# From batch 3 on, queries and keys of a batch's first two pairs are asked for behind the second value part of a pair under way

## The chip, the core and the metric

The kernel runs on one core of one Trainium2 chip. The metric is device microseconds from start to end of one launch; the time of a version is the median of several runs. The core has five engines with their own instruction queues: TensorE (PE, with its weight loads listed as PEld), VectorE (DVE), ScalarE (ACT), GpSimd (POOL) and SyncE (SP). In this kernel every DMA is issued by SP, in the order of SP's program, so a DMA that must wait holds all DMAs behind it.

## The reference

Windowed attention over 8 batches, 8 heads, 576 positions and 64 channels; half of the heads look at the last 32 positions, half at every fourth of the last 128. Its output, 8 x 576 x 512, goes through a mixing layer with cosines and sines.

```python
scores = scale * np.matmul(q, k.transpose(0, 1, 3, 2))
scores = np.where(masks[None, :, :, :], scores, -1000000000.0)
attn = softmax(scores); x = np.matmul(attn, v)      # then heads side by side: (B, S, 512)
theta = x @ w_theta
zr, zi = x * np.cos(theta), x * np.sin(theta)
y = einsum('ts,bsd->btd', w_tok_r, zr) + einsum('ts,bsd->btd', w_tok_i, zi)
u = x + y
out = u + np.maximum(u @ w_ch, 0.0)
```

## The kernel before

**Pairs.** Two heads make a pair; a batch has four pairs, 0 to 3 (`NP` = 4). For a pair the kernel loads queries `q` (576 KB), keys `k` (304 KB) and the values of nine windows in two parts: `va`, the first five windows (320 KB), and `vb`, the last four (256 KB). In the names of tiles the batch comes first: `q4_0` is the queries of batch 4, pair 0. There are two buffers for `q`, `k` and `va`, and **one** for `vb`.

**Steps on TensorE.** `scores(b, pr)` (tile `s`, L547) multiplies queries by keys, and `pv(b, pr)` (tile `o`, L704) multiplies the turned probabilities `pt` by the values: 20 matmul records on `va`, then 16 on `vb`. `theta` (tile `th`) is the product with `w_theta`. The token products of a batch are 14 steps (tiles `A`, `B`, `C`, `D`, L1169) on weights that are held in scratch DRAM as `tw_...` and brought into `wt_g`, `late_wt_a` and `late_wt_b` when their turn comes (576 KB a half). `chan` (tile `c`, L1406) is the product with `w_ch`.

**Phases.** From batch 1 on the work runs in phases. Phase b does the 14 steps of batch b, and between them the attention of batch b+1; then `theta` of batch b+1 and `chan` of batch b. From phase 2 on the order on TensorE is: scores(b+1, 2), step 0 (A), pv(b+1, 0), scores(b+1, 3), steps 1 to 3 (B, A, B), pv(b+1, 1), steps 4 and 5 (A), pv(b+1, 2), scores(b+2, 0), steps 6 to 9 (C, D), pv(b+1, 3), scores(b+2, 1), steps 10 to 13 (C, D), and then `theta` and `chan`. So pv(b+1, 1) and pv(b+1, 2) have two steps between them. Phase 1 has the older, slower token product (tile `y`, L1373) in place of the 14 steps, and beside it POOL and ACT build the weight sums `tw_t1` to `tw_t4` (L1071 to L1094), which SP stores (L1100).

**What sets the order.** The steps are Python generators. Each yields an engine and an estimated cost, or an event that it waits for, and `Order.run` works out from that in which order the instructions are written into the engines' programs. A load is such a generator (`load_qk`, `load_va`, `load_vb`): it becomes due when its buffer is freed in that plan, and takes its place in SP's program by its due time. On the chip the engines keep the program order and wait on semaphores. `load_qk` of the pair two further on is started after `scores` of a pair, `load_vb` of the next pair after `pv`. `od.steady` is true once the phases are planned; `FIRST` is 2.

**Names in the prediction.** `x_store` (L842, L849) writes the attention output transposed to DRAM (`xd`) and reads it back as `xn`, in five parts; the part of 64 rows is used first, by the products at L856. `keep` (L1057) stores two weight sets as `tw_b11` and `tw_b22` in phase 1.

Of the kernel before, what the change touches and what calls it, by code (L numbers as in the profile page):

```python
# [58 lines left out]
FIRST = 2  # L59
# [21 lines left out]
class Order:  # L81
# [14 lines left out]
    def pin(self, ins):  # L96
        if self.live:
            self.tc.keep_in_program_order(ins)

    def signal(self, event):  # L100
        self.events[event] = self.now
# [96 lines left out]
def dma(n):  # L198
    return 128 * 4 * n / 360.0
# [3 lines left out]
def build(ctx, tc, qT, kT, vw, wth, wtk, wch, maskb, ident, identb, outT):  # L203
# [14 lines left out]
    od = Order(tc)  # L218
    pin, go, signal = od.pin, od.go, od.signal
# [16 lines left out]
    def reserve(tag):  # L236
        taken[tag] = taken.get(tag, -1) + 1
        return taken[tag]

    def take(tag, bufs, n=None):  # L240
        n = reserve(tag) if n is None else n
        if od.live:
            if n >= bufs:
                yield None, ("free", tag, n - bufs)
            if n:
                yield None, ("got", tag, n - 1)
            signal(("got", tag, n))
        return n
# [15 lines left out]
    def load_qk(n):  # L264
        if n >= B * NP:
            return
        b, pr = divmod(n, NP)
        yield "rank", due.get(("scores", b, pr), od.rank)
        r = yield from take("qk", 2)
        q = ap.tile([128, 2 * NJ, 2 * QB], F32, tag="q", name=f"q{b}_{pr}")  # L270
        k = ap.tile([128, S + 32], F32, tag="k", name=f"k{b}_{pr}")
        yield "DMA", dma(2 * S)
        pin(nc.sync.dma_start(q, qT[b, pr]))
        yield "DMA", dma(S + 32)
        pin(nc.sync.dma_start(k, kT[b, pr]))
        qks[b, pr] = (q, k, r)
        signal(("qk", b, pr))
# [13 lines left out]
    def load_vb(n):  # L291
        if n >= B * NP:
            return
        b, pr = divmod(n, NP)
        yield "rank", due.get(("pv", b, pr), od.rank)
        if n == NP - 1:
            r = None
            vb = hp.tile([128, DM], F32R, tag="zl8", name="first_vb").bitcast(F32)
            vb = vb.rearrange("p (a b) -> p a b", b=128)
        else:  # L300
            r = yield from take("vb", 1)
            vb = ap.tile([128, NJ - VA, 128], F32, tag="vb", name=f"vb{b}_{pr}", bufs=1)
        yield "DMA", dma((NJ - VA) * 128)
        pin(nc.sync.dma_start(vb, vw[b, pr, :, VA:]))
        vs["b", b, pr] = (vb, r)
        signal(("vb", b, pr))
# [38 lines left out]
    def first_loads():  # L345
        yield "DMA", dma(3 * BW + 64)
        pin(nc.sync.dma_start(mskb, maskb.bitcast(BF16)))
        pin(nc.sync.dma_start(idb, identb.bitcast(BF16)))
        for pr in range(NP):
            yield from take(f"xh{pr}", 1, 0)  # L350
            yield from take(f"u{pr}", 1, 0)
            pqs.append(hp.tile([128, 2, S], F32R, tag=f"xh{pr}", name=f"P0_{pr}").bitcast(F32)[:, 0])
            q = hp.tile([128, 2, S], F32R, tag=f"u{pr}", name=f"q0_{pr}").bitcast(F32)
            q = q.rearrange("p a b -> p (a b)").rearrange("p (a b) -> p a b", b=2 * QB)
            k = first_k[:, KE * pr:KE * pr + KE]
            yield "DMA", dma(2 * S)
            pin(nc.sync.dma_start(q, qT[0, pr]))
            yield "DMA", dma(KE)
            pin(nc.sync.dma_start(k, kT[0, pr]))
            qks[0, pr] = (q, k, None)  # L360
            if pr == 0:
                yield "DMA", dma(128)
                pin(nc.sync.dma_start(idt, ident))
            signal(("qk", 0, pr))
        for pr in range(NP // 2):
            v = first_v[:, NJ * 128 * pr:NJ * 128 * pr + NJ * 128].rearrange("p (a b) -> p a b", b=128)
            yield "DMA", dma(NJ * 128)
            pin(nc.sync.dma_start(v, vw[0, pr]))
            for h, t in (("a", v[:, :VA]), ("b", v[:, VA:])):
                vs[h, 0, pr] = (t, None)  # L370
                signal(("v" + h, 0, pr))
        for pr in range(NP // 2, NP):
            yield from load_va(pr)
            yield from load_vb(pr)
# [143 lines left out]
    def scores(b, pr):  # L518
# [36 lines left out]
        if b == 0:  # L555
            give(f"u{pr}", 0)
        else:
            give("qk", rqk)
            go(load_qk(b * NP + pr + 2), RANK["load"])
# [128 lines left out]
    def pv(b, pr):  # L688
        yield None, ("va", b, pr)
        yield None, ("vb", b, pr)  # L690
        yield None, ("pt", b, pr)
        if pr >= 1:
            yield None, ("pv", b, pr - 1)
        if b > 2:
            yield None, ("stored", b - 2, pr)
        (va, ra), (vb, rb) = vs["a", b, pr], vs["b", b, pr]
        xf[b, pr] = xp.tile([128, S], F32, tag=f"x{pr}", name=f"x{b}_{pr}")
        n = yield from take("v", 1)
        ps = ps_v.tile([128, 2 * DM], F32, tag="v", name=f"o{b}_{pr}")[:, :S]
        yield "PE", 1060 if od.steady else 1300  # L700
        for j in range(NJ):
            v = va[:, j] if j < VA else vb[:, j - VA]
            for hh in range(2):
                pe(nc.tensor.matmul(ps[64 * hh:64 * hh + 64, BW * j:BW * j + BW], v[:, 64 * hh:64 * hh + 64],  # L704
                                    pmats[b, pr][:, j, hh], start=True, stop=True))
        go(x_evac(b, pr, ps, ("v", n), ("xe", b, pr)))
        signal(("pv", b, pr))
        n = b * NP + pr
        if ra is not None:
            give("va", ra)  # L710
            go(load_va(n + 2), RANK["load"])
        if rb is not None:
            give("vb", rb)
            go(load_vb(NP if n == NP - 2 else n + 1), RANK["load"])
        if b:
            go(x_split(b, pr))
# [828 lines left out]
    def second_loads():  # L1545
        for n in (NP, NP + 1):
            yield from load_qk(n)
# [113 lines left out]
```

## Time and profile before

| | |
|---|---|
| median of 3 runs | 564.9 us (564.89 to 566.3) |
| the profiled execution's own time | 562.37 us |
| its span | 560.6 us |
| granted TensorE clock, mean | 0.991 |
| busy share: PE, PEld, DVE, ACT, POOL | 95%, 86%, 78%, 66%, 59% |
| DMA queue of SP, share of 16 engines | 64.8%, 123.49 MB |
| phases 2 to 6, first scores to first scores | 61.74, 62.38, 62.11, 62.04, 59.43 us |

The profiled execution is 2.5 us below the median of the runs, and its span is 1.8 us below its own time; differences are worked out on the span and carried over to the median. Phase 6 is shorter since no batch 8 follows, so it has two score steps fewer and loads no queries and keys. A "busy" share counts instructions in flight, so 95% on PE hides short waits; the chain that ended last and the gaps between PE's rows show them.

### The profile page before, as it was taken

How to read it: one execution, taken by the hardware profiler on the slowest of the kernel's cores; microseconds unless marked ns; L12 is line 12 of the kernel's file. 1: busy time of each engine (PE TensorE's matmuls, PEld its weight loads, DVE VectorE, ACT ScalarE, POOL GpSimd, SP SyncE). 2: the span in 40 equal slices, each digit the busy share in tenths (PEclk: the TensorE clock that was granted, in tenths of full speed). 3: DMA queues.
4: the chain of work that ended last, by engine and by line, in shares of the span. 5: the costliest groups of instructions: out<-in, count | busy, mean ns of one | idle time of the engine just before them, and what ended most of it. 6: DMA issues, size and time to landing. Idle time of an engine off the chain costs nothing.

```text
span 560.6 us, 14386 instructions
## 1 busy us (share of the span) xinstructions
PE 530.9 (95%) x5320; PEld 481.5 (86%) x5320; DVE 434.9 (78%) x1315; ACT 372.4 (66%) x1033; POOL 332.5 (59%) x351
## 2 busy tenths in 40 slices
PE   4897799889998999999999999999999999999997
PEld 3744689778997899998999899998999899989997
DVE  3889799994687787979897997979797997748322
ACT  1598966868748578487776778487767767567220
POOL 2228858788994274763567374655476375727660
PEclk9999799899999999999999999999999999999999
DMA  8991535832659948995499918993599817690622
GB/s 303 400 390 29 177 108 185 256 118 96 201 200 309 317 162 324 322 263 189 141 363 292 307 44 314 324 279 149 199 341 290 276 63 227 213 279 37 211 92 85
DMA packets 59126, 124.41 MB, mean 222 GB/s; under 512 B 5424, under 2 KB 24624, under 8 KB 58800
## 3 DMA queue, kind: packets, MB, share of 16 engines
q1 hardware_dynamic: 59056, 123.49, 64.8%
q8 instruction: 42, 0.69, 0.5%
q14 instruction: 28, 0.23, 0.1%
HBM read 99.88 MB, written 23.59 MB: 220 GB/s over the span
## 4 chain that ended last, share of the span: by engine, by line
PE 70%; DVE 9%; DMA 9%; POOL 5%; ACT 4%; issue 2%; SPq 1%; DVEq 0%; POOLq 0%
PE c L1406 16%; PE th L776 12%; PE C L1169 9%; PE D L1169 7%; PE A L1169 5%; PE B L1169 4%; PE s L547 4%; PE o L704 4%; PE y L1373 4%; DMA vb<-in_vw_dram 4%; DMA st_wtk<-in_wtk_dram 3%; DVE pt L608 3%; POOL z L737 1%; DMA first_k<-in_kT_dram 1%; PE th L781 1%
## 5 line engine op out<-in xcount | busy, mean ns | idle before, releaser
L608 DVE STREAM_TRANSPOSE pt<-P 32x288 f32<-32x288 f32 x224 | 105.2, 470 | 11.8 <-POOL P L590 7.3
L1406 PE MATMUL c<-u,late_wc 128*128 128x288 f32 x768 | 108.3, 295 | 0.0
L1406 PEld LDWEIGHTS c<-u,late_wc 128*128 128x128 f32 x768 | 105.6, 188 | 2.6
L584 ACT ACTIVATE P<-P,mx 128x64 f32<-128x64 f32 x216 | 72.3, 336 | 12.7 <-DVE mx L578 12.5
L776 PE MATMUL th<-wthh,xh 128*128 128x512 f32 x224 | 74.9, 395 | 0.0
L590 POOL TENSOR_TENSOR P<-P,sm 128x576 f32<-128x576 f32 x32 | 39.5, 1235 | 59.0 <-DVE mx L578 29.4
L1187 POOL TENSOR_TENSOR u<-x,u 128x288 fp32r<-128x288 f32 x48 | 40.1, 838 | 20.8 <-ACT u L1185 20.6
L1185 ACT CAST u<-x 128x288 fp32r<-128x288 f32 x48 | 20.5, 427 | 45.0 <-DVE x L1195 45.0
L776 PEld LDWEIGHTS th<-wthh,xh 128*128 128x128 f32 x224 | 42.1, 188 | 9.2
L776 PE MATMUL th<-wthl,xh 128*128 128x512 f32 x112 | 44.3, 396 | 0.0
L486 DVE CUSTOM_DVE_ANT_0 P<-s,mskb 128x64 f32<-128x64 f32 x216 | 33.2, 217 | 14.3 <-PE s L547 14.3
L584 ACT ACTIVATION_READ_ACCUMULATOR P<-P,mx 128x1 f32 x216 | 40.4, 187 | 0.0
L664 ACT COPY x<-o 128x576 f32<-128x576 f32 x32 | 29.5, 921 | 15.0 <-PE o L704 14.9
L737 POOL TENSOR_TENSOR zl<-g,zh 128x512 fp32r<-128x512 f32 x7 | 9.1, 1297 | 48.9 <-ACT zh L735 48.9
L1382 DVE SCALAR_TENSOR_TENSOR x<-c,x 128x288 f32<-128x288 f32 x64 | 28.3, 449 | 12.3 <-PE c L1406 12.2
L547 PE MATMUL s<-k,q 128*64 128x64 f32 x1008 | 36.6, 226 | 0.0
L547 PEld LDWEIGHTS s<-k,q 128*64 128x64 f32 x1008 | 32.8, 140 | 3.7 <-issue 2.7
L704 PEld LDWEIGHTS o<-pt,va 128*64 128x64 f32 x600 | 21.4, 140 | 7.2 <-issue 4.9
L949 POOL TENSOR_TENSOR s<-f,x 128x256 f32<-128x256 f32 x24 | 17.8, 740 | 16.1 <-DVE f L937 13.7
L704 PE MATMUL o<-pt,va 128*64 128x64 f32 x600 | 25.6, 230 | 1.7 <-ACT pt L622 1.2
L1373 PE MATMUL y<-wt_g,z 128*128 128x288 f32 x96 | 20.7, 320 | 6.7 <-POOL z L737 4.1
L776 PEld LDWEIGHTS th<-wthl,xh 128*128 128x128 f32 x112 | 21.0, 188 | 4.0
(245 smaller groups left out, 1609.4 us busy)
## 6 DMA issues: line engine op xcount, KB each, us to landing
q<-in_qT_dram SPq DMA_DIRECT2D x32, 576.0 KB, 5.8
late_wt_a<-tw_t SPq DMA_DIRECT2D x24, 576.0 KB, 6.2
wt_g<-tw_b SPq DMA_DIRECT2D x22, 576.0 KB, 6.1
va<-in_vw_dram SPq DMA_DIRECT2D x30, 320.0 KB, 5.6
k<-in_kT_dram SPq DMA_DIRECT2D x28, 304.0 KB, 6.0
out_dram<-x SPq DMA_DIRECT2D x28, 288.0 KB, 2.1
vb<-in_vw_dram SPq DMA_DIRECT2D x29, 256.0 KB, 4.5
xd<-xq SPq DMA_DIRECT2D x24, 288.0 KB, 5.3
```

The costliest lines, as they stand in the source:

```text
L486: pin(nc.vector.tensor_tensor_reduce(out=P[:, n], in0=ps[:, n - g0], in1=mskb[:, mask_of(pr, n)], op0=ALU.add, op1=ALU.max, scale=1.0, sca ...
L547: pe(nc.tensor.matmul(ps[64 * e:64 * e + 64, n - g0], q[:, qb], k[:, QB * qb:QB * qb + BW], start=not masked, stop=not masked or n == g1 - 1))
L584: table(nc.scalar.activation(P[:, n], P[:, n], AF.Exp, bias=mx[:, n:n + 1], scale=SCALE, accum_out=sm[:, n:n + 1]))
L590: pin(nc.gpsimd.tensor_tensor(P, P, sm.unsqueeze(2).to_broadcast([128, NJ, BW]), op=ALU.mult))
L608: pin(nc.vector.transpose(pmats[b, pr][k0:k0 + QB, :, hh, QB * e:QB * e + QB], P[p0:p0 + QB, :, QB * o:QB * o + QB]))
L664: pin(nc.scalar.copy(dst, src))
L704: pe(nc.tensor.matmul(ps[64 * hh:64 * hh + 64, BW * j:BW * j + BW], v[:, 64 * hh:64 * hh + 64], pmats[b, pr][:, j, hh], start=True, stop=T ...
L776: pe(nc.tensor.matmul(pt, l, r, start=(n == 0), stop=(n == 3 * NC - 1)))
L1169: pe(nc.tensor.matmul(ps, l, r, start=first and n == 1, stop=last and n == 3 * len(ks), skip_group_check=more))
L1187: pin(nc.gpsimd.tensor_tensor(ul[b, d][:, ts], x[:, ts], uh[b, d][:, ts].bitcast(F32), op=ALU.subtract))
L1373: pe(nc.tensor.matmul(ps, l[:, cs], r, start=(n == 0), stop=(n == 3 * NK - 1)))
L1406: pe(nc.tensor.matmul(ps, l[:, cs], r[:, ts], start=(n == 0), stop=(n == 3 * NC - 1)))
```

## The change

A load of queries and keys for pair 0 or 1 of batch 3 or later, after its buffer number is given out, now also waits in the plan until `load_vb` of (batch before, pair + 1) has taken the `vb` buffer. So `q4_0` and `k4_0` are planned behind `vb3_1`, and `q4_1` and `k4_1` behind `vb3_2`. No instruction is added or taken away, and no buffer changes; the change acts only through the order in which `Order.run` writes the programs.

```diff
         r = yield from take("qk", 2)
+        if od.steady and b > FIRST and pr < 2:
+            yield None, ("vbi", b - 1, pr + 1)
         q = ap.tile([128, 2 * NJ, 2 * QB], F32, tag="q", name=f"q{b}_{pr}")
...
             r = yield from take("vb", 1)
+            signal(("vbi", b, pr))
             vb = ap.tile([128, NJ - VA, 128], F32, tag="vb", name=f"vb{b}_{pr}", bufs=1)
```

The order on PE stays as it was. SP's order changes in phases 1 to 5, and DVE, ACT and POOL change theirs at the end of phase 1 alone. The added lines move later line numbers by 2 or 3.

**SP, first part of phase 2** (phases 3, 4 and 5 move alike). Before:

```order
L273 DMA q4_0_2779<-in_qT_dram 128x1152
L275 DMA k4_0_2780<-in_kT_dram 128x608
L1051 DMA wt_g_90<-tw_t3_1491 128x1152
L304 DMA vb3_1_2840<-in_vw_dram 128x512
L287 DMA va3_2_2839<-in_vw_dram 128x640
L273 DMA q4_1_2865<-in_qT_dram 128x1152
L275 DMA k4_1_2866<-in_kT_dram 128x608
L1051 DMA wt_g_90<-tw_t3_1491 128x1152
L304 DMA vb3_2_2972<-in_vw_dram 128x512
L287 DMA va3_3_2971<-in_vw_dram 128x640
L1051 DMA late_wt_a_788<-tw_t4_1529 128x1152 x2
```

And now:

```order
L1054 DMA wt_g_90<-tw_t3_1491 128x1152
L307 DMA vb3_1_2836<-in_vw_dram 128x512
L289 DMA va3_2_2835<-in_vw_dram 128x640
L275 DMA q4_0_2837<-in_qT_dram 128x1152
L277 DMA k4_0_2838<-in_kT_dram 128x608
L1054 DMA wt_g_90<-tw_t3_1491 128x1152
L307 DMA vb3_2_2968<-in_vw_dram 128x512
L289 DMA va3_3_2967<-in_vw_dram 128x640
L275 DMA q4_1_2969<-in_qT_dram 128x1152
L277 DMA k4_1_2970<-in_kT_dram 128x608
L1054 DMA late_wt_a_788<-tw_t4_1529 128x1152
L307 DMA vb3_3_3046<-in_vw_dram 128x512
```

`q4_0` and `k4_0` moved from ahead of `vb3_1` to behind `va3_2`, `q4_1` and `k4_1` from ahead of `vb3_2` to behind `va3_3`; further on `q4_2` and `k4_2` went behind the two halves of `tw_b22`, and `va4_1` behind `k4_3`.

**SP in phase 1, around the last value part of batch 2** (`tx`, `ta`, `tb`, `tc`, `td` are the tiles in which POOL and ACT leave the weight sums). Before:

```order
L1100 DMA tw_t3_1491<-tb_1803 128x288
L1100 DMA tw_t3_1491<-ta_1802 128x288
L1100 DMA tw_t2_1511<-tx_102 128x288 x2
L1100 DMA tw_t2_1511<-tc_1804 128x288
L1100 DMA tw_t2_1511<-tb_1803 128x288
L1100 DMA tw_t4_1529<-tx_102 128x288
L1100 DMA tw_t4_1529<-td_1805 128x288
L1100 DMA tw_t4_1529<-ta_1802 128x288
L304 DMA vb2_3_2163<-in_vw_dram 128x512
L1100 DMA tw_t4_1529<-tx_102 128x288
L273 DMA q3_2_2194<-in_qT_dram 128x1152
```

And now:

```order
L277 DMA k3_1_2022<-in_kT_dram 128x608
L1103 DMA tw_t3_1491<-tb_1803 128x288
L1103 DMA tw_t3_1491<-ta_1802 128x288
L1103 DMA tw_t3_1491<-tx_102 128x288
L1103 DMA tw_t2_1511<-tc_1804 128x288
L1103 DMA tw_t2_1511<-tb_1803 128x288
L1103 DMA tw_t3_1491<-tx_102 128x288
L1103 DMA tw_t4_1529<-td_1805 128x288
L1103 DMA tw_t4_1529<-ta_1802 128x288
L307 DMA vb2_3_2161<-in_vw_dram 128x512
L1103 DMA tw_t2_1511<-tx_102 128x288 x2
L1103 DMA tw_t4_1529<-tx_102 128x288 x2
```

`k3_1` now stands among the stores (`q3_1` three rows above it), and of the stores from `tx` three more stand behind `vb2_3` than before.

**SP at the end of phase 1, the return of the attention output of batch 2.** Before:

```order
L273 DMA q3_3_2312<-in_qT_dram 128x1152
L842 DMA xd2_2321<-xq2_2220 32x18x128 x4
L275 DMA k3_3_2313<-in_kT_dram 128x608
L849 DMA xn2_2421<-xd2_2321 64x512
L1057 DMA tw_b11_2484<-wt_g_90 128x2304
L1057 DMA tw_b22_2505<-late_wt_b_994 128x2304
L849 DMA xn2_2421<-xd2_2321 128x512 x4
```

And now:

```order
L275 DMA q3_3_2310<-in_qT_dram 128x1152
L845 DMA xd2_2324<-xq2_2235 32x18x128 x4
L277 DMA k3_3_2311<-in_kT_dram 128x608
L289 DMA va3_1_2278<-in_vw_dram 128x640
L1060 DMA tw_b11_2480<-wt_g_90 128x2304
L1060 DMA tw_b22_2503<-late_wt_b_994 128x2304
L852 DMA xn2_2423<-xd2_2324 64x512
L852 DMA xn2_2423<-xd2_2324 128x512 x4
```

The read of the 64-row part of `xn2` moved behind the two stores of 1152 KB each, `tw_b11` and `tw_b22`.

## The prediction

> **What bounds the kernel now.** I read the page first, then who waits for whom on PE, then the chain that ended last phase by phase, and last SP's rows with the time from issue to landing of single DMAs.
>
> ```profile
> span 560.6 us, 14386 instructions
> PE 530.9 (95%) x5320; PEld 481.5 (86%) x5320; DVE 434.9 (78%) x1315; ACT 372.4 (66%) x1033; POOL 332.5 (59%) x351
> PE 70%; DVE 9%; DMA 9%; POOL 5%; ACT 4%; issue 2%; SPq 1%; DVEq 0%; POOLq 0%
> PE o L704 <- DMA vb<-in_vw_dram: 3.7, 5, 2.2
> ```
>
> PE bounds the kernel, and its own work stays as it is. What the change can touch is the last row: `pv` waits five times for `vb`, 3.7 us in all, the longest 2.2 us. A gap between PE's rows understates a stall, since matmuls overlap, so I measure it on the chain. There each phase from 2 to 6 has the same piece: step 4 and 5 (A, 24 records), then pv(b+1, 2), then what follows.
>
> ```profile
> 223.26 3.38 PE A L1169 x24
> 226.65 1.56 PE o L704 x36
> ...
> 285.04 4.82 DMA vb<-in_vw_dram
> 290.58 1.05 PE s L547 x36
> ...
> 300.20 1.05 PE s L547 x36
> ...
> 347.44 4.54 DMA vb<-in_vw_dram
> 352.71 1.05 PE s L547 x36
> ...
> 409.53 4.49 DMA vb<-in_vw_dram
> 414.75 1.05 PE s L547 x36
> ...
> 471.53 3.38 PE A L1169 x24
> 474.92 1.35 PE o L704 x36
> ```
>
> In phases 3, 4 and 5 the chain leaves PE and runs over the DMA of `vb`, issued the moment pv(b+1, 1) frees the only buffer. From that moment to the end of pv(b+1, 2) it is 4.95 us in phase 2 (226.65 + 1.56 - 223.26), 5.54 in phase 3 (290.58 - 285.04), 5.27 in phase 4, 5.22 in phase 5, and 4.74 in phase 6 (474.92 + 1.35 - 471.53). Phase 6 loads no queries and keys, so it is the price without them. Above it stand 0.21, 0.80, 0.53 and 0.48 us: 2.02 us in four phases.
>
> The latest time at which `vb` costs nothing is read from PE's own rows:
>
> ```profile
> 289.89 0.69 PE L704 MATMUL o<-pt,vb 128*64 128x64 f32 x16 [0.62 <-DMA vb<-in_vw_dram]
> ...
> 475.53 0.22 PE L704 MATMUL o<-pt,vb 128*64 128x64 f32 x1
> ```
>
> In phase 6 the first matmul on `vb` starts 4.0 us after the issue (475.53 - 471.57, row below). In phase 3 it starts 0.04 us after the landing (285.04 + 4.82 = 289.86).
>
> **Why `vb` lands late.** SP's rows of phase 3, and of phase 6 last:
>
> ```profile
> 276.39 0.53 SPq L273 DMA_DIRECT2D q<-in_qT_dram  x1
> 276.98 0.46 SPq L275 DMA_DIRECT2D k<-in_kT_dram  x1
> 277.53 0.38 SPq L1051 DMA_DIRECT2D wt_g<-tw_t  x1
> 278.00 0.38 SPq L304 DMA_DIRECT2D vb<-in_vw_dram  x1
> 278.44 0.80 SPq L287 DMA_DIRECT2D va<-in_vw_dram  x1
> 279.32 0.43 SPq L273 DMA_DIRECT2D q<-in_qT_dram  x1
> 279.80 0.46 SPq L275 DMA_DIRECT2D k<-in_kT_dram  x1
> 282.24 0.33 SPq L1051 DMA_DIRECT2D wt_g<-tw_t  x1
> 285.04 0.33 SPq L304 DMA_DIRECT2D vb<-in_vw_dram  x1
> ...
> 471.57 0.33 SPq L304 DMA_DIRECT2D vb<-in_vw_dram  x1
> ```
>
> And the time to landing (last number, us) of single issues: the `q` of 276.39, the `k` of 279.80, the `wt_g` of 282.24, and the `vb` of 471.57 in phase 6.
>
> ```profile
> q<-in_qT_dram SPq DMA_DIRECT2D x1, 576.0 KB, 4.3
> k<-in_kT_dram SPq DMA_DIRECT2D x1, 304.0 KB, 8.0
> wt_g<-tw_t SPq DMA_DIRECT2D x1, 576.0 KB, 7.0
> vb<-in_vw_dram SPq DMA_DIRECT2D x1, 256.0 KB, 2.6
> ```
>
> So they land at 280.7, 287.8, 289.2, and the `vb` of 285.04 at 289.86: in the order of issue, a queue. From 280.7 to 289.86 seven DMAs behind the first `q` and the last `vb` itself land: 304 + 576 + 256 + 320 + 576 + 304 + 576 + 256 = 3168 KB in 9.2 us, 345 KB a microsecond. With nothing queued `vb` takes 2.6 us.
>
> **The change, part by part.**
>
> *Phases 2 to 5, `q` and `k` of the first pair behind `vb` and `va`, those of the second behind the next `vb`.* The same transfers run, but ahead of the `vb` of 285.04 there is now one `q` and `k` instead of two, 880 KB less: 880 / 345 = 2.55 us. Worked out forward: `wt_g` goes first and lands where the first `q` did, 280.7; `vb`, `va`, `q`, `k` (1456 KB, 4.2 us) by 284.9; the second `wt_g` (1.7 us) by 286.6; `vb` by 287.3, and not before 285.04 + 2.6 = 287.6. The deadline is 285.04 + 4.0 = 289.0, so 1.4 us are to spare and the stall goes. Phases 2, 4 and 5 were less late and have the same queue. Term: -2.02 us. If pv(b+1, 2) came down to the 1.20 us that the chain gives every other `pv` of a phase, it would be 0.15 more in each of four phases, -2.6 in all; I don't take that, since phase 6 keeps its 1.35 though its `vb` landed at 474.2, before it was needed. The other end is 0 (rival 1).
>
> *What is late next there.* `q` and `k` of the first pair are issued at about 279 to 280, as the second pair's were, and their slowest landing before was 8.0 us: 287.8, with scores at 290.58 now and about 289.8 then. Cover of 2 us at the old backlog, 4.5 at the new one (284.9): cost 0. Those of the second pair are issued behind `va` at about 286, land by 294 at the slowest, and their scores start at 300.20 in phase 3. Cost 0. `late_wt_a`, 880 KB further back, is read at step 10 still later, and its second half now also stands behind the wait of `vb3_3` on pv(b+1, 2); both are past by 291. `q` and `k` of the third pair now wait behind both halves of `tw_b22` (the end of step 7), some 4 us later for work of the next phase, which is 40 us off. `va` of the second pair moves behind `xn`, again for a use some 30 us off.
>
> *Phase 1, `vb2_3` among the stores.* pv(2, 3) has the longest stall of all:
>
> ```profile
> 165.72 1.74 SPq L1100 DMA_DIRECT2D tw_t<-tc  x1
> ...
> 169.51 0.40 SPq L304 DMA_DIRECT2D vb<-in_vw_dram  x1
> ...
> 167.07 1.26 POOL L1094 TENSOR_TENSOR ta<-ta,td 128x288 fp32r<-128x288 f32 x1
> ...
> 169.63 0.80 PE L704 MATMUL o<-pt,va 128*64 128x64 f32 x20 [0.51 <-ACT x L664]
> 172.63 0.69 PE L704 MATMUL o<-pt,vb 128*64 128x64 f32 x16 [2.19 <-DMA vb<-in_vw_dram]
> ```
>
> `vb2_3` was issued at 169.51 and landed 3.1 us later. It stays behind the store of `ta`, which waits for POOL until 167.07 + 1.26 = 168.33. Then follow `ta` and `vb`, at half a microsecond an issue: 168.9 at best, if SP isn't behind. It may be: the 1.74 us of the `tc` issue can come again (its cause isn't in the trace), and then `vb` goes out at about 169.6. Three stores fewer stand ahead, but 880 KB of `q3_1`, `k3_1` now run in this stretch. Landing 2.6 to 3.1 us after the issue: 171.5 to 172.7, against 172.6. The term lies between -1.1 and +0.1; I take -0.5, the middle.
>
> *End of phase 1, the 64-row part of `xn2` behind 2304 KB of stores.* This is the part that can cost:
>
> ```profile
> tw_b<-late_wt_b SPq DMA_DIRECT2D x1, 1152.0 KB, 7.8
> ...
> 193.94 0.68 DVE L856 TENSOR_TENSOR g<-xn,th 64x512 f32<-64x512 f32 x1
> 204.37 0.69 DVE L856 TENSOR_TENSOR x<-xn,th 128x512 f32<-128x512 f32 x1 [0.29 <-ACT f L911]
> ...
> 203.07 7.99 PE c L1406 x60
> ```
>
> The second store was issued at 185.95, so it landed at 193.8; the part of `xn2` now lands right behind it, 194.2 to 194.9, where DVE read it at 193.94 before. DVE may stand still up to 1.0 us. Behind it on DVE are the sums on `c` and the products that free PSUM banks; the nearest need is the bank that the third `chan` unit of the last run takes: it starts two units behind 203.07, 7.99 / 5 = 1.6 us each, at 206.3, and the product that frees its bank ended at 204.37 + 0.69 = 205.1. Cover 1.2 us, so cost 0; at the upper end 0.8 us, if the stores take 1 us longer. The swaps on DVE, ACT and POOL there move no work in or out.
>
> **Sum.** -2.0 - 0.5 + 0 = -2.5 us: 562.4 becomes 559.9 in the profiled execution. It stands 2.5 us below the median of the runs, 564.9, so the median goes to 562.4, 0.44% less. About 0.3%, 1.7 us, is what a measurement of this kernel can tell from no change.
>
> **Rivals.**
>
> *1. The stall stays, since `vb` is slowed by load and not by the queue ahead of it.* In the two microseconds before its issue the `vb` would meet the same load as before: one `wt_g` under way, and a `q` and `k` just landed or landing. If 4.2 to 4.8 us is what a load under traffic takes, nothing is won in phases 2 to 5 and only phase 1 counts: 564.4. For it: in phase 2 `vb` came late by just 0.2 us although SP had issued the same list. Against it: the landings in order of issue at an even rate. The Trainium skill ("DMA: Bandwidth & Descriptors", Latency and other measured facts) says that the access time of HBM is 0.2 us on average and 2 us at high load, and that a lighter load makes the fixed cost of a DMA smaller. By that rule the 2.2 us between 2.6 and 4.8 could be load alone, and would stay; no run here yet holds the load and takes away the queue.
>
> *2. Slower: `xn2` comes back late.* If the part of `xn2` lands after 193.94 + 1.2 = 195.1, PE waits for a bank microsecond for microsecond. Faster turns to no gain at 197.6, and slower by over 0.3% at 199.3 and later, a median of 566.6 or more. The stores would have to take 13 us instead of 7.8. Against it: DVE's gaps there, and that the 2304 KB had landed by 193.8.
>
> *3. The stall goes in part,* because the second `wt_g` and `q`, `k` still stand ahead: half of -2.0 and -0.5 gives 563.4, no change by the measurement.
>
> **How the numbers follow.** The forecast has 0.70: it spans -3.7 (2.6 + 1.1) to -1.1 with the turn of phase 1 lost and a small loss at `xn2`; in some 0.10 of it the gain stays under 1.7 us. Rival 1 has 0.12, rival 3 0.11, both within 0.3%; rival 2 has 0.07. So faster 0.60, same 0.33, slower 0.07. The range runs from 564.9 - 3.7 = 561.2, with 0.4 for the spread of the three runs (1.4 us between them), to rival 1 at 564.4 with as much: 560.8 to 564.9.
>
> **What would show it.** Right: no row of the chain over `vb` in phases 2 to 5, step 4 to the end of pv(b+1, 2) at 4.74 us in each, `vb` landing 2.6 to 3.5 us after its issue. Phase 1: the gap of 2.19 us smaller, `vb2_3` issued before 169.5. Right too: no gap on PE between 200 and 215, and no wait of scores for `q` or `k`. Wrong: `vb` landing 4 us or more after its issue in phases 2 to 5 (rivals 1 and 3), a wait of DVE for `xn` over 1.2 us (rival 2), or a new wait of `scores` on SP's order.

## The result and the profile after

The changed kernel takes 562.36 us (median of 5 runs, 562.07 to 562.72), the kernel before 565.6 us (5 runs, 564.89 to 566.3). The ratio is 0.9945, with a 95% interval of 0.993 to 0.9959: 0.55% or 3.2 us faster, where 562.4 us and 2.5 us less were forecast. A second set of runs of the changed kernel, beside other kernels, gave 0.9932 (0.9908 to 0.9956).

The profiled execution hardly shows it: its span is 560.4 us, that of before was 560.6. So the phases have to be read apart. From the page: the span, PE's load, and the chain by engine; then who made `pv` wait.

```profile
span 560.4 us, 14371 instructions
PE 80%; DVE 9%; ACT 4%; DMA 3%; POOL 1%; issue 1%; SPq 0%; DVEq 0%
...
PE o L707 <- DMA vb<-in_vw_dram: 2.5, 2, 1.6
```

The page counts 15 instructions fewer than before, none of them of PE, DVE, ACT or POOL (5320, 1315, 1033 and 351 both times). DMA fell from 9% to 3% of the chain, and `pv` waits for `vb` twice instead of five times, both times ahead of phase 2. The chain of the changed kernel at steps 4 and 5 (A), and at what follows pv(b+1, 2), phases 2 to 6:

```profile
225.29 3.38 PE A L1172 x24
...
230.02 1.05 PE s L550 x35
...
286.81 3.38 PE A L1172 x24
...
291.53 1.05 PE s L550 x35
...
348.32 3.38 PE A L1172 x24
...
353.06 1.05 PE s L550 x35
...
409.85 3.38 PE A L1172 x24
...
414.59 1.05 PE s L550 x35
...
471.38 3.38 PE A L1172 x24
...
476.12 4.17 PE C L1172 x30
```

No row over `vb` is left. The piece takes 4.73, 4.72, 4.74, 4.74 and 4.74 us; before it was 4.95, 5.54, 5.27, 5.22 and 4.74. From first scores to first scores phases 2 to 5 now take 61.52, 61.51, 61.53 and 61.53 us, together 246.09; before 61.74, 62.38, 62.11 and 62.04, together 248.27. That is 2.18 us. The changed profile had lost nearly as much ahead of phase 2: its first scores there start at 213.09 us, those of before at 211.06. The second profile of the kernel before, below, shows that this stretch differs by as much without any change.

### The profile page after: what moved, and what is told of

Same layout as the page of the kernel before. It is cut to its first block, busy times and chain, and to the rows that moved or that the text cites. A ratio compares the mean times of both kernels' runs of the same rounds, so it can differ in the third digit from the quotient of the medians.

```text
span 560.4 us, 14371 instructions
## 1 busy us (share of the span) xinstructions
PE 533.9 (95%) x5320; PEld 484.9 (87%) x5320; DVE 434.0 (77%) x1315; ACT 372.2 (66%) x1033; POOL 332.5 (59%) x351
## 4 chain that ended last, share of the span: by engine, by line
PE 80%; DVE 9%; ACT 4%; DMA 3%; POOL 1%; issue 1%; SPq 0%; DVEq 0%
PE c L1409 17%; PE th L779 13%; PE C L1172 9%; PE y L1376 7%; PE D L1172 7%; PE A L1172 7%; PE s L550 6%; PE o L707 5%; PE B L1172 4%; DVE pt L611 2%; DMA vb<-in_vw_dram 1%; PE th L784 1%; DMA st_wch<-in_wch_dram 1%; DMA first_k<-in_kT_dram 1%; PE th L783 1%
## 5 line engine op out<-in xcount | busy, mean ns | idle before, releaser
L550 PE MATMUL s<-k,q 128*64 128x64 f32 x1008 | 38.0, 230 | 0.0
L550 PEld LDWEIGHTS s<-k,q 128*64 128x64 f32 x1008 | 34.2, 144 | 3.6 <-issue 2.0
```

Source lines behind the costliest of these rows:

```text
L550: pe(nc.tensor.matmul(ps[64 * e:64 * e + 64, n - g0], q[:, qb], k[:, QB * qb:QB * qb + BW], start=not masked, stop=not masked or n == g1 - 1))
```

## The experiments

### The kernel before, profiled again

No edit.

> The kernel before, unchanged, profiled a second time. Its first profiled execution took 562.37 us where its runs have a median of 565.6 us, so that one execution cannot carry a difference of 2 to 3 us. If the first 210 us vary from execution to execution (clock, first loads) and phases 2 to 5 do not, this profile shows again 61.7, 62.4, 62.1 and 62.0 us for phases 2 to 5, and its difference to the first one lies ahead of the first scores of phase 2. If instead the stalls on vb vary, they are longer here and the phases with them.

Measured: phases 2 to 5 took 62.32, 61.74, 62.93 and 62.27 us, together 249.26, and `vb` of (b+1, 2) landed 4.8, 4.2, 5.1 and 4.7 us after its issue. Both parts of the expectation hold in half: the stalls do vary, from 2.0 us in the first profile to 2.9 in this one, and the stretch ahead varies more. pv(2, 0), in phase 1, starts at 148.40 us in the first profile of before, at 150.81 in the second, at 149.46 in that of the changed kernel, and between 148.35 and 150.81 in the others, for programs whose order is the same up to there. The granted clock between 168 and 182 us was 1.00 in the first profile of before and 0.88 in this one and in the changed kernel's; from pv(2, 0) to the first scores of phase 2 the same program took 62.66 us in the first and 64.14 in this one. So the first profile was a short execution, with a short stall: 246.09 against 249.26 is 3.2 us for phases 2 to 5 alone. The runs of before in this series reach from 561.7 to 567.8 us, so medians are told with their intervals, and the phases decide.

### Which pair's loads matter

Pair 1 alone:

```diff
-        if od.steady and b > FIRST and pr < 2:
+        if od.steady and b > FIRST and pr == 1:
```

> Only queries and keys of pair 1 wait for the second value part; those of pair 0 stay where they were before. Theory (a queue: what counts is how much SP has asked for ahead of vb of (b+1, 2)): 880 KB less stand ahead of it, as with the whole change, so vb lands under 4.0 us after its issue, the piece from step 4 to the end of pv(b+1, 2) takes 4.74 us in phases 2 to 5, and the time is that of the whole change, 562.4 us, within 0.7. Rival (what helps is that the first pair's q and k no longer stand ahead of vb of (b+1, 1)): the stall stays as before, about 565.

Measured: ratio 0.9945 (0.992 to 0.997), and 0.9946 (0.9927 to 0.9965) in a second set. The landing of `vb` of (b+1, 2), phases 2 to 5:

```profile
vb<-in_vw_dram SPq DMA_DIRECT2D x1, 256.0 KB, 2.8
vb<-in_vw_dram SPq DMA_DIRECT2D x1, 256.0 KB, 2.6
vb<-in_vw_dram SPq DMA_DIRECT2D x1, 256.0 KB, 2.8
vb<-in_vw_dram SPq DMA_DIRECT2D x1, 256.0 KB, 2.8
```

For this stall half of the change does all of it, and `vb` lands earlier than under the whole change.

Pair 0 alone is the same line with `pr == 0`.

> Only queries and keys of pair 0 wait; q of pair 1 is asked for just ahead of vb of (b+1, 2), k of pair 1 behind it. Theory (queue): against the whole change 576 KB more stand ahead of that vb; at 345 KB a microsecond it lands up to 1.7 us later than the 3.7 us of the whole change, 4.5 to 5.4 us, so 0.5 to 1.4 us are lost in each of phases 3 to 5, and the time is 564 to 566 us, no better than before by more than 0.3%. Rival (the first pair's place is what helps): as fast as the whole change, 562.4.

Measured: ratio 1.0003 (0.9982 to 1.0024). `vb` landed 5.2, 5.4, 4.5 and 4.7 us after its issue. In the chain of its phase 3:

```profile
287.50 5.44 DMA vb<-in_vw_dram
292.94 0.04 issue
292.98 0.69 PE o L707 x16
293.67 1.05 PE s L550 x36
```

6.17 us from the issue to the next scores, 1.47 over the 4.70 that phase 6 of before takes from its issue (4.74 from the start of step 4, 0.04 us earlier). The `q` of the second pair stood just ahead of `vb`, and the stall is no smaller than before. This run also had two waits of 0.6 us of PE on a sum of DVE at the start of phase 2, which the other orders do not show. The queue's account holds; that the first pair's place is what helps is refuted.

### Phases 2 to 5 alone

```diff
-        if od.steady and b > FIRST and pr < 2:
+        if od.steady and b > FIRST + 1 and pr < 2:
```

> The change for batches 4 to 7 only, so phases 2 to 5 have it and phase 1 has the order of before. Theory: 2.0 to 2.2 us of the gain stay, the 0.5 us of phase 1 go: 562.9 us, with the gap of 2.2 us ahead of pv(2, 3) back. Rival (the measured 3.2 us is more than 2.0 + 0.5 since phase 1 gives more than 0.5 in a usual run): 563.5 or more.

Measured: ratio 0.9954 (0.9932 to 0.9975), 562.48 us. Phases 2 to 5 took 61.53, 61.53, 61.52 and 61.73 us, and the gap in phase 1 was back at 2.43 us. So nearly all of the gain comes from phases 2 to 5. What phase 1 adds is below what the medians tell (562.48 against 561.76 to 562.36 for the whole change). The gap's own rows, 2.19 and 2.17 us before and 1.65 and 1.82 after, differ by 0.4 to 0.5 us; whether the stretch got shorter by as much is taken up under phase 1 below.

### Ahead of `vb` or behind it

```diff
+        if od.steady and b > FIRST and b < B - 1 and pr == 2:
+            spare = dp.tile([128, 17, 2 * QB], F32, tag="spare", name=f"spare{b}", bufs=4)
+            pin(nc.sync.dma_start(spare, qT[b, 3, :, :17]))
         pin(nc.sync.dma_start(vb, vw[b, pr, :, VA:]))
```

> The changed kernel with one spare copy of 544 KB, from DRAM to DRAM, asked for just ahead of vb of (b+1, 2) in phases 2 to 5; nothing reads the copy. Theory (queue): vb lands 544 / 345 = 1.6 us later, 5.3 us after its issue in phases 3 to 5 (3.7 now) and 4.4 in phase 2 (2.8 now), so over the 4.0 us that cost nothing stand 1.3 us in three phases and 0.4 in one: about 4.3 us more than the changed kernel, 566.7 us. Rival (load, not the queue): vb is slowed by what runs beside it, ahead or behind alike; then this kernel and the one with the copy behind vb take the same.

For the other kernel the same three lines stand behind the load of `vb`.

> The same spare copy of 544 KB, but asked for right behind vb of (b+1, 2). Theory (queue): vb lands as in the changed kernel, 3.7 us after its issue in phases 3 to 5 and 2.8 in phase 2, nothing is lost: 562.4 us, within 0.7. Rival (load): vb is slowed as much as with the copy ahead, some 4 us are lost.

Measured, SP's rows of phase 3 with the copy ahead, then with the copy behind, and under each the landing of its `vb`:

```profile
285.85 0.53 SPq L309 DMA_DIRECT2D spare<-in_qT_dram  x1
288.27 0.33 SPq L310 DMA_DIRECT2D vb<-in_vw_dram  x1
...
vb<-in_vw_dram SPq DMA_DIRECT2D x1, 256.0 KB, 4.7
```

```profile
286.32 0.33 SPq L307 DMA_DIRECT2D vb<-in_vw_dram  x1
286.70 0.64 SPq L310 DMA_DIRECT2D spare<-in_qT_dram  x1
...
vb<-in_vw_dram SPq DMA_DIRECT2D x1, 256.0 KB, 3.8
```

Over phases 2 to 5 it landed after 5.2, 4.7, 5.0 and 4.7 us with the copy ahead, after 2.8, 3.8, 3.3 and 3.7 us with the copy behind. The phases took 249.83 us together in the one, 246.22 in the other: 3.6 us between the same bytes in two places, where 4.3 was expected (`vb` landed 0.9 to 2.4 us later than with the copy behind, not 1.6 throughout). The medians, 565.22 and 563.52 us, lie the same way, but their intervals overlap (0.9945 to 1.0004 and 0.994 to 0.9984), and neither is the expected one: 1.5 us below 566.7, and 1.1 above 562.4, which was given within 0.7. So the phases decide. What SP asks for right behind `vb` costs it nothing; what SP has asked for ahead of it does. The copy behind landed 5.4 us after its issue in phase 3, at 292.1, 2.0 us after `vb`, so much of it moved when `vb` was done: the pair tests the order of asking, and says less of traffic that moves at the very same time.

### A place of its own for `vb` of (2, 3)

```diff
+        elif n == 3 * NP - 1:
+            r = None
+            vb = hp.tile([128, 2 * S], F32R, tag="xh3", name="third_vb").bitcast(F32)
+            vb = vb[:, :DM].rearrange("p (a b) -> p a b", b=128)
...
-            go(load_vb(NP if n == NP - 2 else n + 1), RANK["load"])
+            go(load_vb(n + 2 if n in (NP - 2, 3 * NP - 2) else n + 1), RANK["load"])
+            if n == 2 * NP:
+                go(load_vb(3 * NP - 1), RANK["load"])
```

> The changed kernel, and the vb of (2, 3) gets a place of its own, in the buffer of xh3 that lies idle until pv(2, 3) is done, so that it is asked for behind pv(2, 0) and not behind the stores of the weight sums in phase 1; vb of (3, 0) then takes its turn after pv(2, 2). Theory: the gap of 1.65 us ahead of the vb part of pv(2, 3) goes and nothing else comes, 560.8 us. Rival: another wait takes its place (the turned probabilities, or the weight sums, whose loads the earlier vb delays), within 0.5 us of the changed kernel.

The changed kernel beside it:

> The changed kernel again, beside the three above on the same chip: 562.4 us, within 0.5, for their differences.

Measured: 561.51 us (ratio 0.9918, 0.9888 to 0.9948), the changed kernel 561.76 us (0.9932, 0.9908 to 0.9956). The expected 560.8 us was not reached. The gap of phase 1 is gone; PE's waits between 140 and 530 us in this kernel are these two, and the first is not new (0.99 us in the changed kernel's profile of this set):

```profile
PE o L711 <- ACT x L671: 1.0, 1, 1.0
PE o L711 <- DMA vb<-in_vw_dram: 0.5, 1, 0.5
```

From pv(2, 0) to step 0 of phase 2 it takes 62.15 us (150.81 to 212.96) against 63.90 (148.35 to 212.25) in the changed kernel's profile of this set, both at a clock of 1.00 between 168 and 182 us: 1.75 us. Against the two kernels with the copy, at the same clock, it is 1.8 and 1.2 us (63.96 and 63.34). The medians differ by 0.25 us, which is as near as the rival had it, but tells nothing where executions differ by more ahead of pv(2, 0). The wait of 0.5 is a late `vb` in phase 5, 4.7 us after its issue; the changed kernel had one of 4.5 us in the same phase of this set, and the kernel with phases 2 to 5 alone one of 4.2. The whole change thus sits at its deadline, and over it in phase 5 of three of the four profiles with its order there and no copy.

### Both: pair 1 alone, and the place for `vb` of (2, 3)

> Only pair 1 waits, and the vb of (2, 3) has the idle buffer of xh3. Theory (a queue with a deadline of 4.0 us): vb of (b+1, 2) lands 2.6 to 2.8 us after its issue in phases 2 to 5 as with pair 1 alone, each phase takes 61.5 us, and the gap of 1.5 us ahead of the vb part of pv(2, 3) is gone: 1.5 us less than with pair 1 alone, about 560.5 us. Rival: the timed runs differ by more than that through their first 150 us, so it can't be told from the pair-1 kernel by the median, only by the phases of the profile.

> Pair 1 alone a second time, beside the kernel above: 562 us, vb of (b+1, 2) landing 2.6 to 2.9 us after its issue in all four phases, where the whole change showed 2.8 to 4.5 us in its two profiles. If a landing over 4 us shows up here too, the margin of pair 1 alone is chance.

Measured: 560.11 us, ratio 0.9908 (0.9878 to 0.9938), the lowest of the study; pair 1 alone 562.31 us. `vb` of (b+1, 2) landed after 3.3, 2.7, 2.7 and 2.8 us, with pair 1 alone after 2.6, 2.7, 2.7 and 3.5: one in each later than expected, none over 4 us. But pair 1 alone leaves `q` and `k` of pair 0 ahead of `vb` of (b+1, 1), and that one lands as late as before the change (4.8 to 6.5 us after its issue in the first profile of before, 3.7 to 4.2 in the changed kernel's). In phase 2 of the combined kernel it took 6.7 us from its issue at 216.10, and PE waited.

```profile
vb<-in_vw_dram SPq DMA_DIRECT2D x1, 256.0 KB, 6.7
...
222.84 0.34 PE L711 MATMUL o<-pt,vb 128*64 128x64 f32 x4 [0.68 <-DMA vb<-in_vw_dram]
```

In the second profile of before it took 6.4 us in phase 4 and stands in the chain there. So the half for pair 0 is not idle: it trades margin at pv(b+1, 2) for margin at pv(b+1, 1).

## Why the prediction was right, point by point

**The stall of phases 2 to 5: right.** 2.02 us were forecast, 2.18 gone. The working counts phases 3 to 5 from the issue of the DMA, but phases 2 and 6 from the start of step 4, 0.04 us earlier; counted alike, the stalls are 0.21, 0.84, 0.57 and 0.52 us, 2.14 in all. Phase 6 was the right base: the piece came down to its 4.74 us and not to the 1.20 us of other `pv`s. The deadline of 4.0 us held throughout. The table gives, for phases 2 to 5, us from issue to landing of `vb` of (b+1, 2), and what the piece took over 4.74, all counted from the start of step 4.

| kernel | landing | over 4.74 |
|---|---|---|
| before | 4.2, 4.8, 4.5, 4.5 | 0.21, 0.84, 0.57, 0.52 |
| before, second profile | 4.8, 4.2, 5.1, 4.7 | 0.79, 0.21, 1.12, 0.74 |
| changed | 2.8, 3.7, 3.8, 3.6 | 0, 0, 0, 0 |
| changed, second profile | 3.1, 3.5, 4.0, 4.5 | 0, 0, 0, 0.5 |
| pair 1 alone | 2.8, 2.6, 2.8, 2.8 | 0, 0, 0, 0 |
| copy of 544 KB ahead | 5.2, 4.7, 5.0, 4.7 | 1.2, 0.7, 1.0, 0.8 |

**The landing itself: mis-sized.** The forward working said 2.6 us after the issue in phase 3 and 1.4 us to spare; it was 3.7, with 0.3 to spare. The sign for right, 2.6 to 3.5 us, was missed in phases 3 to 5, and the sign for wrong, 4 us or more, came in two phases of the second profile. Of the working's steps, the first `wt_g` came as forecast. SP's rows and the landings behind them:

```profile
278.16 0.65 SPq L1054 DMA_DIRECT2D wt_g<-tw_t  x1
279.63 0.34 SPq L307 DMA_DIRECT2D vb<-in_vw_dram  x1
...
284.05 0.33 SPq L1054 DMA_DIRECT2D wt_g<-tw_t  x1
286.84 0.33 SPq L307 DMA_DIRECT2D vb<-in_vw_dram  x1
```

The four landings are 4.2, 3.8, 4.7 and 3.7 us after the issue. The phase starts 1.81 us later than before (274.61 against 272.80). By the clock of before the first `wt_g` landed at 280.6 (forecast 280.7), the second at 286.9 (288.75 less 1.81; forecast 286.6), and `vb` at 288.7 (forecast 287.6): 1.8 us behind the `wt_g`, where a queue at 345 KB a microsecond gives 0.74. That distance is not a fixed one: it is 0.6 us in phases 2 and 5 of the same profile, where the `wt_g` itself landed 2.2 and 3.0 us after the issue of `vb` instead of 1.6, and 0.6 to 0.7 in phases 2 to 5 before. So the rate of 345 KB a microsecond, an average over 9.2 us of a full queue, was too coarse a term for the last two transfers; what sets their distance stays open. The cover took it up. A likely cause of the thin margin is seen in pair 1 alone: there SP sends `q` and `k` of pair 0 at once, 3.5 us into the phase, while in the changed kernel it first stands still for pv(b+1, 0) with `vb` at the head of its queue (278.16 + 0.65 to 279.63), and sends them 5.9 us into the phase.

**Phase 1: right in the gap, unclear in the time.** -0.5 was taken between -1.1 and +0.1. The gap went from 2.19 to 1.65 us. SP's and PE's rows:

```profile
168.33 1.25 SPq L1103 DMA_DIRECT2D tw_t<-td  x1
169.67 0.38 SPq L1103 DMA_DIRECT2D tw_t<-ta  x1
170.15 0.40 SPq L307 DMA_DIRECT2D vb<-in_vw_dram  x1
...
173.16 0.69 PE L707 MATMUL o<-pt,vb 128*64 128x64 f32 x16 [1.65 <-DMA vb<-in_vw_dram]
```

This execution is 1.06 us late at pv(2, 0), so `vb` went out at 169.1 by the clock of before, between the 168.9 and 169.6 of the two cases. The long issue did come again, at `td`; its cause stays open. The gap is 2.17 to 2.43 us in the three profiles with the old order of phase 1, and 1.46 to 2.04 in the six with the new one (whole change, pair 1 alone and the copies). In the time of the stretch it is less clear: from pv(2, 0) to step 0 of phase 2, at a granted clock of 1.00 between 168 and 182 us, it took 63.79 and 64.02 us with the old order, 63.90, 63.96 and 63.34 with the new one; at 0.88 it took 65.27 with the old, 64.76, 64.48 and 65.15 with the new. The averages differ by 0.2 and 0.5 us, and the same order differs by up to 0.7 from profile to profile. So the -0.5 of the sum is borne out for the wait, and as time it is not shown.

**`xn2` behind the stores: cost right, wait misread.** DVE was to stand still up to 1.0 us for the part of `xn2`; it stood 2.0, for something else. The timeline of the changed kernel:

```profile
193.99 0.69 ACT L920 ACTIVATE cos<-f,halfpi 64x512 f32<-64x512 f32 x1
...
195.79 0.69 ACT L920 ACTIVATE cos<-f,halfpi 128x512 f32<-128x512 f32 x1
...
196.51 0.68 DVE L859 TENSOR_TENSOR g<-xn,cos 64x512 f32<-64x512 f32 x1 [1.98 <-ACT cos L920]
```

The landings there:

```profile
tw_b<-late_wt_b SPq DMA_DIRECT2D x1, 1152.0 KB, 9.1
...
xn<-xd SPq DMA_DIRECT2D x1, 128.0 KB, 9.0
```

The stores took 9.1 us instead of 7.8, so the part, issued at 186.15, landed at 195.15 instead of by 194.9: alone that would have held DVE for 0.6 us. But DVE went on only at 196.51, 0.03 us behind the second `cos`, whose data this product does not use. The written order of DVE there, before and after, with the waits of each row:

```
354 L856 TENSOR_TENSOR g_8_2468<-xn_2421,th_4_2456 64x512 [waits DMAHW6_49]
355 L856 TENSOR_TENSOR g_8_2468<-xn_2421,cos_2467 64x512 [waits DVE_49,Activation_49]
356 L902 SCALAR_TENSOR_TENSOR x_2_2471<-th_1_2522,x_2_2471 128x512 [waits Activation_49]
357 L937 TENSOR_TENSOR cos_2467<-xn_2421,cos_2467 128x256 [waits DMAHW1_49,DVE_49]

353 L859 TENSOR_TENSOR g_8_2467<-xn_2423,cos_2466 64x512 [waits DMAHW0_49,DVE_49,Activation_49]
354 L859 TENSOR_TENSOR g_8_2467<-xn_2423,th_4_2456 64x512
355 L1385 SCALAR_TENSOR_TENSOR x_1_1031<-c_1_0_2535,x_1_1031 128x288 [waits PE_49]
356 L940 TENSOR_TENSOR cos_2466<-xn_2423,cos_2466 128x256 [waits DMAHW1_49,DVE_49]
```

Row 356 reads the second `cos` and has no wait on ACT of its own: row 353 already waits far enough. In all seven profiles with this order (whole change, pair 1, pair 0, both copies) the gap is 1.98 us and ends with that `cos`, while the part of `xn2` lands 0.7 to 2.3 us earlier; in the five where the load stands ahead of the stores (before twice, phases 2 to 5 alone, the place for `vb`, both) neither product has a gap. So the wrong step of the forecast was "The swaps on DVE, ACT and POOL there move no work in or out": no work was moved, but the swap made a wait. PE did not feel it: from the first full `theta` run to the first scores of phase 2 it took 23.91 us (189.18 to 213.09), as before (187.15 to 211.06). The 1.2 us of cover were worked out for one bank in the order of before; why 2.0 cost nothing was not tested. The cover has an end: with pair 0 alone, where the scores of phase 2 come 61.10 us after pv(2, 0) and not 62.70 as in the changed kernel at the same clock, PE waited twice, 0.59 and 0.56 us, for DVE's sums on `c`. Whether the gap of 1.98 us caused that was not tested.

**Rivals.** Rival 1 (load, not the queue) is refuted by the copy ahead and behind. By that rival the copy behind would have cost 4 us; phases 2 to 5 took 246.22 us with it against 246.09 without. The Trainium skill ("DMA: Bandwidth & Descriptors", Latency and other measured facts) states that HBM access time grows at high load; these runs do not show it. Rival 3 did not come in the first profile, and shows a trace of itself in the second (4.5 us in phase 5, 0.5 us lost). Rival 2 went its way without reaching its point.

**The total.** 3.2 us measured against 2.5 forecast, within the interval of 2.3 to 4.0. That the forecast median of 562.4 us was met to 0.1 is luck: it started from 564.9 where the kernel before came to 565.6, and the gain is larger by as much. The likely reason is that the forecast was made on an execution with small stalls: 2.0 us, where the second profile of before has 2.9. The second profile of the changed kernel has 246.61 us for phases 2 to 5, so the two pairs of profiles give 2.2 and 2.7 us there. Two profiles do not make this a proof.

## What to carry to other kernels

A buffer with a single copy gives its load a deadline: here 4.0 us from the moment it is freed. Work out how much the queue holds ahead of that load at that moment, and put behind it what has more time; but do not put a load that must still wait at the head of a queue in front of loads that could go. And read an expected gain in the phase where it arises, over more than one execution: the whole span moved by 0.2 us in the first pair of profiles, and the phases by 2.2.

## What the runs showed of the hardware

The gap ahead of a matmul understates its stall: 0.62 us in the row of phase 3 before, where the piece lost 0.84, and none in phase 2, where it lost 0.21. And a load of 256 KB took 2.6 us to 5.4 us at the same place of the same phase, by what the one queue held ahead of it, while 544 KB asked for 0.4 us behind it left it as it was.
